# A retention block feeding a gated MLP on one core: the first unit in two parts, a 128-row product for the decay rows, and another order of the first block with more work on GpSimd

## The chip, the cores and the metric

The kernel runs on one core of one Trainium2 chip. The metric is the time of one execution on the device in microseconds (us); the times given are medians of several runs. A profile is one further execution recorded by the hardware profiler. Its engines are PE (TensorE matmuls; PEld are its weight loads), DVE (VectorE), ACT (ScalarE), POOL (GpSimd) and SP (SyncE, which here only issues transfers). Each engine works through its own instructions in order.

## The reference

```python
# q, k, v: (4, 8, 768, 64) float32
gamma = 1.0 - 2.0 ** (-5.0 - np.arange(H))
for t in range(S):
    state = gamma[None, :, None, None] * state + einsum('bhd,bhe->bhde', k[:, :, t], v[:, :, t])
    y[:, :, t] = (1 / np.sqrt(D)) * einsum('bhd,bhde->bhe', q[:, :, t], state)
x = y.transpose(0, 2, 1, 3).reshape(3072, 512)      # one row per token
h = x @ w_in                                        # w_in (512, 2048), w_out (2048, 512)
return (h * (1.0 / (1.0 + np.exp(-1.702 * h)))) @ w_out
```

The recurrence over 768 tokens per head, with a decay per head, is followed by an MLP with a sigmoid-gated hidden layer. All is float32; the two weight matrices arrive as 64-bit words (float64) and are narrowed to float32 on the chip.

## The kernel before

**Retention in steps.** Tokens are worked in steps of 64, for two batches at once and all 8 heads; a step is written with its number, `j`. For a step, q and k are turned on PE by an identity product (`turn_q`, `turn_k`, L283; the copies out of PSUM are `turned_q`, `turned2_q`, `turned_k`, L300). `score` (L339) forms the products of keys and queries, `masked` (L380, VectorE) multiplies them with a mask of decays, `gain` (L347) forms the step's own addition to the state from the decayed keys (`decay`: L318 on GpSimd, or L323 on ScalarE in eight instructions, one per head), `past` (L358) the part of the old state, and `own` (L367) the part of the step itself. `state` (by_state, L387) and `x` (output, L409) put both parts together into the MLP's input, in the tile X. `aged` (L418 on VectorE or GpSimd, L421 on ScalarE in four instructions) and `updated` (L432) carry the state on. Four steps make a block of MLP rows; the first eight steps, two blocks, are what the change concerns.

**Weights.** Each 128-column pair of `w_in` comes in as two halves of raw 64-bit words by SyncE (`w3a`, `w3b`; L201) into a ring of three slots, and is narrowed by six works: `abs` (L237) and `low` (L241) on ScalarE, `clip` (L245), `lift` (L248), `sign` (L253) and `rest` (L258) on VectorE. A slot of the ring is loaded again when `low` and `sign` of its last weight are done. `w0` to `w7` are of `w_in`, `w8` to `w15` of `w_out`.

**The MLP of the first block.** A unit `up0.th.p` (up0, L476) is the product of weight pair `p` with half `th` of the block's rows: eight matmuls of 256 columns. Half 0 is the rows of steps 0 and 1, half 1 those of steps 2 and 3, so the unit waits for `x1` or `x3`. `gate` (hidden, L457) is ScalarE's sigmoid product. Later units of block 0 (`zero`, L559) and block 1 (`seven`, L599) use a scheme of seven products with sums of the operands: `zero_x` (L546) and `seven_x` (L500) make four sums of X each, one building on another, on VectorE; `seven_4`, `seven_6`, `seven_52` make the sums of weights, and `seven_keep` (L538) writes some of them to DRAM on SyncE's queue.

**The order.** All these works stand in one list of names (L1105 to L1127). `works[name]` issues the work, a suffix as `@pool` names the engine, and within each engine the instructions run in the order of the list (`pin` keeps it, L124). SyncE's and GpSimd's transfers stand in their queues in the same order, and a transfer into a buffer that is still read waits there and holds all behind it. `zN` is `N` dummy matmuls of 512 bfloat16 columns (keep_warm, L1011) whose results nobody reads. `rows` (L1017) spreads the row of decays over 128 partitions by one matmul with a column of ones: one partition of `ones` (L104) times one partition of `row` (L103). `mask`, `causal` and `rowd` are made from its result. `table` loads ScalarE's table for the sigmoid. From the third block on, the loop at L1138 orders the work; the change does not touch it.

## Time and profile before

| | us |
|---|---|
| median of 3 runs | 649.44 (648.33 to 653.43) |
| the profiled execution | 651.44 |
| its span, first to last instruction | 649.7 |
| PE busy | 633.4 |
| VectorE busy | 435.6 |
| ScalarE busy | 184.4 |
| GpSimd busy | 152.0 |

The span is counted from the first instruction; the execution's own time has 1.74 us around it. Busy time is the union of an engine's instructions. A matmul of float32 appears as two passes, so a unit of eight matmuls shows as x16. "Idle before" with a releaser tells what an engine waited for, as far as the semaphores show it. The granted clock of TensorE stands in the column PEclk of a table of stretches; 1.00 there also stands for stretches without a record of the clock.

### The profile page before, as it was taken

The numbers are of one execution on the slowest core, as the hardware profiler recorded it, in microseconds if no ns is written. First come the engines' busy times: TensorE is split into PE (matmuls) and PEld (weight loads), VectorE is DVE, ScalarE is ACT, GpSimd is POOL, SyncE is SP. The second block draws the span as 40 slices with busy tenths as digits, with TensorE's granted clock in tenths as the row PEclk, the third lists the DMA queues.
The fourth block names the chain that finished last, engine by engine and source line by source line (L and its number), as shares of the span: only waits on it lengthen the run. The fifth ranks groups of instructions, "written<-read, shape, count | busy, mean of one in ns | idle before, by whom it ended". The sixth has DMA issues, their size and how long they took to land.

```text
span 649.7 us, 15510 instructions
## 1 busy us (share of the span) xinstructions
PE 633.4 (97%) x6543; PEld 578.4 (89%) x6543; DVE 435.6 (67%) x643; ACT 184.4 (28%) x329; POOL 152.0 (23%) x184
## 2 busy tenths in 40 slices
PE   7899999999999998999999999999999999999997
PEld 4788888888889997889999889999888999888997
DVE  2879887979989962438874337985246976145854
ACT  3778237661001102332101333100333110233210
POOL 4000211300612435000645000635300425200000
PEclk9989999999999999999999999999999999999999
DMA  9995587783368875720667730667741354221143
GB/s 198 228 258 161 112 252 214 198 209 57 93 200 264 206 175 171 200 67 4 172 179 213 215 85 1 160 161 189 211 95 49 89 174 143 110 91 49 59 153 98
DMA packets 150710, 96.86 MB, mean 149 GB/s; under 512 B 130512, under 2 KB 135888, under 8 KB 149616
## 3 DMA queue, kind: packets, MB, share of 16 engines
q1 hardware_dynamic: 138048, 42.83, 30.2%
q0 software_dynamic: 8672, 40.00, 19.3%
q10 hardware_dynamic: 3920, 13.04, 5.4%
q8 instruction: 51, 0.84, 0.6%
q14 instruction: 19, 0.16, 0.1%
HBM read 79.18 MB, written 14.94 MB: 145 GB/s over the span
## 4 chain that ended last, share of the span: by engine, by line
PE 83%; DMA 9%; SPq 5%; issue 1%; DVE 1%; ACT 1%; ACTq 0%
PE pq L821 33%; PE px L698 17%; PE pz L698 9%; PE pd L954 7%; PE ph L599 6%; PE py L698 4%; DMA W<-in_moe_w_out_dram 2%; SPq L161 2%; PE pa L339 2%; DMA q_in<-in_q_dram 2%; DMA kn_in<-in_k_dram 2%; DMA LATE<-W1D 1%; SPq L176 1%; PE py L367 1%; PE pa L347 1%; DMA v_in<-in_v_dram 1%
## 5 line engine op out<-in xcount | busy, mean ns | idle before, releaser
L821 PE MATMUL pq<-W,G 128*128 128x128 f32 x840 | 100.3, 276 | 0.0
L821 PEld LDWEIGHTS pq<-W,G 128*128 128x128 f32 x840 | 97.0, 192 | 0.8
L796 POOL DMA_DIRECT2D LATE<-W2D x34 | 18.7, 551 | 260.5 <-PE pq L821 139.8
L821 PE MATMUL pq<-LATE 128*128 128x128 f32 x560 | 74.8, 277 | 0.0
L821 PEld LDWEIGHTS pq<-LATE 128*128 128x128 f32 x560 | 68.2, 192 | 0.6
L698 PE MATMUL px<-X,LATE 128*128 128x256 f32 x256 | 60.6, 380 | 2.2 <-DMA LATE<-W1D 2.2
L698 PE MATMUL px<-X,W1A 128*128 128x256 f32 x256 | 60.5, 379 | 0.0
L698 PEld LDWEIGHTS px<-X,LATE 128*128 128x128 f32 x256 | 48.6, 190 | 9.1 <-issue 2.6
L698 PEld LDWEIGHTS px<-X,W1A 128*128 128x128 f32 x256 | 48.4, 190 | 6.3
L743 DVE TENSOR_TENSOR G<-pz,vv 128x512 f32<-128x512 f32 x16 | 11.1, 692 | 51.5 <-ACT vv L713 51.5
L843 ACT ACTIVATE o<-pq 128x512 f32<-128x512 f32 (+1 forms) x18 | 9.8, 544 | 119.9 <-PE pq L821 94.3
L457 ACT ACTIVATE G<-G 128x512 f32<-128x512 f32 x49 | 30.9, 630 | 43.1 <-DVE G L753 19.7
L821 PE MATMUL pq<-LATE,G 128*128 128x128 f32 x280 | 37.0, 275 | 0.0
L821 PE MATMUL pq<-W,LATE 128*128 128x128 f32 x280 | 37.0, 275 | 0.0
L954 PE MATMUL pd<-W,LATE 128*128 128x256 f32 x160 | 35.1, 380 | 0.0
L821 PEld LDWEIGHTS pq<-W,LATE 128*128 128x128 f32 x280 | 34.1, 192 | 0.0
L821 PEld LDWEIGHTS pq<-LATE,G 128*128 128x128 f32 x280 | 34.1, 192 | 0.0
L954 PEld LDWEIGHTS pd<-W,LATE 128*128 128x128 f32 x160 | 30.4, 190 | 4.1
L683 DVE TENSOR_TENSOR G<-G 128x512 f32<-128x512 f32 (+2 forms) x28 | 15.9, 567 | 23.5 <-ACT G L457 23.5
L810 DVE TENSOR_TENSOR LATE<-G 128x512 f32<-128x512 f32 x35 | 27.6, 789 | 5.0 <-PE pq L821 2.2
L476 PE MATMUL ph<-X,W1A 128*128 128x256 f32 x128 | 30.6, 397 | 0.2 <-DVE X L409 0.2
L698 PE MATMUL pz<-X,W1A 128*128 128x256 f32 x128 | 30.3, 380 | 0.0
(214 smaller groups left out, 1163.5 us busy)
## 6 DMA issues: line engine op xcount, KB each, us to landing
LATE<-W2D POOLq DMA_DIRECT2D x34, 768.0 KB, 5.2
W<-in_moe_w_out_dram SPq DMA_DIRECT2D x12, 512.0 KB, 6.0
LATE<-W1D ACTq DMA_DIRECT2D x4, 1536.0 KB, 9.7
LATE<-W1D POOLq DMA_DIRECT2D x4, 1536.0 KB, 8.9
kn_in<-in_k_dram SPq DMA_DIRECT2D x84, 64.0 KB, 4.8
W<-in_moe_w_in_dram SPq DMA_DIRECT2D x10, 512.0 KB, 4.8
out_dram<-o POOLq DMA_DIRECT2D x20, 256.0 KB, 4.6
q_sq<-in_q_dram SPq DMA_DIRECT2D x144, 32.0 KB, 3.0
```

Source lines behind the costliest of these rows:

```text
L161: keep(engine.dma_start(t[r * D:(r + 1) * D, i * HP:(i + 1) * HP], src[b + i, r * HP:(r + 1) * HP, rows, :].rearrange("h p d -> p h d")))
L339: pe.matmul(PAS[HALF[w], u, 0, s, :], kt[HALF[u], w, s, :], qt[HALF[u], w, s, :], start=True, stop=True)
L457: pin(act.activation(g, h[:, i], AF.Gelu_apprx_sigmoid))
L476: pe.matmul(h[:, ab], w, X[:, 2 * th + c // 2, c % 2, :], start=(ab == 0 and c == 0), stop=(c == 3), skip_group_check=True)
L599: pe.matmul(acc[:, u, :], w, x, start=(start and u == 0 and c == 0), stop=(stop and c == 1), skip_group_check=True)
L683: hold(dve.tensor_sub(q[0][1], q[0][0], q[0][1]))
L698: pe.matmul(acc[:, u, :], w1(2 * d + u, sw)[:, c, :], X[:, sx, c, :], start=(start and u == 0 and c == 0), stop=(stop and c == 1), skip_gr ...
L743: dve.tensor_add(a[3], z, v)
L796: engine.dma_start(c, W2D[i])
L810: dve.tensor_add(d[:, 0], s2, a11)
L821: pe.matmul(p0[:, j, :], a[:, d], w[:, d], start=(new and j == 0 and d == 0), stop=(d == NP // 2 - 1), skip_group_check=True)
L954: pe.matmul(p0[:, n, :], g1(m, p, sa)[:, n * P:(n + 1) * P], W2[:, sb, p, :], start=(new and p == 0 and n == 0), stop=(last and p == NP - ...
```

## The change

- The first unit, `up0.0.2`, is cut by steps. `firstb` and `firsta` (new function `up0_first`) multiply the rows of step 0 alone with the second and the first halves of the weight pair, 64 columns for each of two batches, eight matmuls of 128 columns. `up0.0.2` itself does the same for step 1. Both go into the same PSUM tile.
- `row` and `ones` have 128 partitions. Two blocks of G are set to zero first, and the row is loaded into partition 0, so that the product in `rows` contracts over 128 partitions of which 127 add zeros.
- The order of the list is another one, above all in its first third. q0 is issued first; `rows` stands behind `turn_k0`; `z5` becomes `z4` behind `turn_q0`, and `z1 z4` are added ahead of `own1`; `mask` and `causal` stand behind `turn_q1`; w0b goes ahead of q1, k3 ahead of v2, w3a ahead of q3; w11a goes behind `seven_keep.2`, and `updated7` some way back.
- Engines: `decay0` from GpSimd to ScalarE; `decay2` to `decay5` from ScalarE to GpSimd; `aged2` from VectorE and `aged4` from ScalarE to GpSimd; `aged5` from ScalarE to VectorE; `zero_x` and `seven_x` from VectorE to GpSimd; `rowd` from ScalarE to VectorE; `updated0` and `turned2_q1` from VectorE to ScalarE.

The new words `both` and the tuple of engines in `load` are not used by the list. In the instruction streams both parts of the first unit stand directly behind one another on PE, behind `turn_q2`, and ScalarE has a table load ahead of its first copy as well as the one of `table`.

```diff
@@ -100,8 +100,8 @@
     G0 = one.tile([P, 2, TH], F32, name="g0", tag="kd")
     X1 = W2[:, 6].rearrange("p (s c) t -> p s c t", s=4)
     rowd = const.tile([P, HP, D], F32, name="rowd")
-    row = G[0:1, 4, 0:2].rearrange("p a (h t) -> p (a h) t", t=D)
-    ones = G[0:1, 4, 2, 0:P]
+    row = G[:, 4, 0:2].rearrange("p a (h t) -> p (a h) t", t=D)
+    ones = G[:, 4, 2, 0:P]
     cold = const.tile([P, 2 * H], F32, name="cold")
     whole = const.tile([P, HP], F32, name="whole")
     whole_h = const.tile([P, H], F32, name="whole_h")
@@ -155,7 +155,8 @@
                 if j < NEW:
                     to, at = t[i * D:(i + 1) * D], src[b + i, :, rows, :].rearrange("h p d -> p h d")
                     for n in range(1 if name == "v" else 2):
-                        keep(engine.dma_start(*((to, at) if name == "v" else (to[:, n:H:2], at[:, n * HP:(n + 1) * HP]))))
+                        by = engine[n] if isinstance(engine, tuple) else engine
+                        keep(by.dma_start(*((to, at) if name == "v" else (to[:, n:H:2], at[:, n * HP:(n + 1) * HP]))))
                 else:
                     for r in range(2):
                         keep(engine.dma_start(t[r * D:(r + 1) * D, i * HP:(i + 1) * HP],
@@ -467,8 +468,25 @@
     def g1(m, p, s):
         return g(m, p // 2 * 2, s)[:, p % 2]
+    FIRST = []
+
+    def up0_first(half, t=0):
+
+        if not FIRST:
+            FIRST.append(ps.tile([P, 2, TH], F32, name="ph", tag="x"))
+        h = FIRST[0].rearrange("p ab (i t) -> p ab i t", i=2)
+        x = X.rearrange("p s c (i t) -> p s c i t", i=2)
+        for ab in range(2):
+            for c in (2, 3) if half else (0, 1):
+                pe.matmul(h[:, ab, :, t:t + D], W1A[:, 2, 2 * ab + half, c % 2, :], x[:, half, c % 2, :, t:t + D],
+                          start=(t == 0 and half == 1 and ab == 0 and c == 2), stop=(half == 0 and c == 1), skip_group_check=True)
+
     def up0(th, p, tag):
+        if (th, p) == (0, 2):
+            for half in (1, 0):
+                up0_first(half, D)
+            return W1L[:, p, 0:2].rearrange("p s c f -> p (s c f)"), FIRST[0]
         h = ps.tile([P, 2, TH], F32, name="ph", tag=tag)
         for ab in range(2):
             for c in range(4):
@@ -491,13 +509,13 @@
     SUM_X, SUM_W = {}, {}
-    def seven_x():
+    def seven_x(engine=dve):
         for n, tag in ((4, "q_sq"), (5, "q_sq"), (6, "k_sq"), (2, "k_sq")):
             SUM_X[n] = two.tile([P, 2, TH], F32, name=f"x{n}", tag=tag)
         for to, a, b in ((SUM_X[4], X1[:, 2], X1[:, 0]), (SUM_X[5], X1[:, 3], SUM_X[4]),
                          (SUM_X[6], X1[:, 3], X1[:, 2]), (SUM_X[2], X1[:, 1], SUM_X[5])):
-            pin(dve.tensor_sub(to, a, b))
+            pin(engine.tensor_sub(to, a, b))
     def seven_4(d):
@@ -540,10 +558,10 @@
     SUM_0 = {n: W2[:, i, NP - 2:NP] for i, n in enumerate((4, 5, 6, 2))}
-    def zero_x():
+    def zero_x(engine=dve):
         for n, a, b in ((4, X[:, 2], X[:, 0]), (5, X[:, 3], SUM_0[4]), (6, X[:, 3], X[:, 2]), (2, X[:, 1], SUM_0[5])):
-            pin(dve.tensor_sub(SUM_0[n], a, b))
+            pin(engine.tensor_sub(SUM_0[n], a, b))
     ZERO = {}
@@ -1003,6 +1021,7 @@
                 bass.AP(tensor=col_decay.tensor, offset=col_decay.offset, ap=[[W, D], [D * W + H, 2], [1, H]])))
         make_identity(nc, ident)
         dve.memset(flow, 1.0)
+        dve.memset(G[:, 4, 0:2], 0.0)
         dve.memset(ones, 1.0)
         dve.memset(first, 0.0)
@@ -1057,7 +1076,7 @@
         "table": lambda: pin(act.activation(first, first, AF.Gelu_apprx_sigmoid)),
         "mask": lambda: pin(dve.tensor_mul(m3, products["rows"], cold[:, 0:H, None].to_broadcast([P, H, D]))),
-        "causal": causal, "rows": rows, "row": lambda engine=pool: pin(engine.dma_start(row, row_decay[None, :, 0:D])),
+        "causal": causal, "rows": rows, "row": lambda engine=pool: pin(engine.dma_start(row[0:1], row_decay[None, :, 0:D])),
         "rowd": lay_rowd, "whole": lay_whole, "late_loads": late_loads, "anew": halves_anew,
         } | {f"z{n}": lambda n=n: keep_warm(n) for n in range(1, 33)}
     for j in range(2 * CB):
@@ -1070,6 +1089,7 @@
         works[f"turned2_q{j}"] = lambda *e, j=j: turned(j, 0, *(e or (act,)), 1)
         works |= {f"turned_{name}{j}": lambda *e, j=j, n=n: turned(j, n, *e) for n, name in enumerate("qk")}
     works |= {f"pace{n}": lambda n=n: PACE.append(n) for n in range(1, 17)}
+    works |= {"firstb": lambda: up0_first(1), "firsta": lambda: up0_first(0)}
     works |= {"seven_x": seven_x, "zero_x": zero_x}
     for d in range(NP // 2):
         works |= {f"seven_{n}.{d}": lambda d=d, do=do: do(d)
@@ -1103,31 +1123,32 @@
     begin()
     for name in """
-        row@sp k0@act table q0 v0 z5 rows turn_q0 turn_k0 q1 w0b k1@sp w0a mask causal turned_q0
-        turned2_q0@dve turned_k0 decay0@pool score0 v1 turn_k1 turn_q1 masked0 gain0 turned_k1 turned_q1 turned2_q1@dve own0 abs0b low0b updated0
-        decay1@pool score1 clip0b lift0b sign0b rowd whole q2 k2@sp masked1 abs0a low0a rest0b x0 past1 gain1
-        clip0a lift0a sign0a own1 rest0a aged1 turn_k2 turn_q2 w2b w2a state1 updated1 x1 turned_k2 turned_q2 turned2_q2@dve
-        v2 q3 k3@sp up0.0.2 score2 abs2 decay2 aged2@dve q4 clip2 lift2 sign2 low2 decay3 w3b w3a
-        masked2 turn_k3 turn_q3 k4@sp gain2 past2 own2 v3 q5 rest2 k5@sp gate0.0.2 turned_k3 turned_q3 turned2_q3@dve updated2
-        state2 score3 decay4 low3 turn_q4 turn_k4 up0.0.3 x2 masked3 gain3 past3 own3 abs3 clip3 lift3 sign3
-        turned_q4 turned2_q4@dve rest3 turned_k4 score4 turn_k5 turn_q5 up0.0.6 w1a w5b w1b aged3 updated3 state3 w5a v4
-        x3 up0.1.3 turned_q5 turned2_q5@dve gate0.0.3 abs1 low1 abs5 clip1 aged4 lift1 sign1 masked4 own4 gain4 w6a
-        rest1 clip5 lift5 gate0.0.6 sign5 up0.0.7 past4 w6b decay5 low5 rest5 updated4 v5 gain5 w4a abs6
-        gate0.1.3 turned_k5 clip6 state4 x4 lift6 score5 masked5 w4b abs4 up0.1.7 low6 aged5 gate0.0.7 w7a w7b
-        low7 low4 q6 sign6 v6 own5 rest6 past5 seven_4.2 state5 gate0.1.7 seven_6.2 updated5 zero2.0 clip4 up0.1.6
-        lift4 sign4 x5 seven_52.2 rest4 turn6 anew decay6 abs7 aged6 up0.1.2 w8a gate0.1.2 clip7 zero_x zero2.1
...
-        w9a updated6 aged7 gate0.1.6 zero2.5 decay7 zero2.6 state6 w11a seven_4.0 x6 zero0.0 score7 masked7 abs8 clip8
-        past7 zero0.1 state7 seven_6.0 seven_52.0 lift8 sign8 gain7 own7 x7 seven_x zero0.2 zero0.3 zero0.4 zero0.5 low8
-        seven_keep.2 w9b abs9 low11 clip9 rest8 lift9 zero0.6 w10a seven2.0 w10b seven2.1 abs11 clip11 lift11 sign11
...
+        k0@act whole q0 row@sp v0 w0b q1 turn_q0 z4 turn_k0 rows k1@sp w0a turned_q0 table turned2_q0@dve
+        turned_k0 decay0@act score0 v1 turn_k1 turn_q1 mask causal masked0 abs0b gain0 low0b clip0b lift0b sign0b turned_k1
+        turned_q1 turned2_q1@act own0 rest0b updated0@act decay1@pool score1 rowd@dve q2 k2@sp masked1 x0 gain1 low0a z1 z4
+        own1 abs0a clip0a lift0a sign0a rest0a aged1 turn_k2 past1 turn_q2 w2b w2a state1 x1 k3@sp firstb
+        firsta up0.0.2 updated1 turned_k2 turned_q2 turned2_q2@dve v2 w3a q3 decay2@pool aged2@pool q4 score2 abs2 clip2 lift2
+        sign2 low2 turn_k3 turn_q3 k4@sp decay3@pool w3b masked2 gain2 past2 own2 v3 q5 rest2 k5@sp gate0.0.2
+        turned_q3 turned_k3 turned2_q3@dve updated2 decay4@pool state2 low3 turn_q4 turn_k4 score3 up0.0.3 x2 masked3 gain3 past3 abs3
+        clip3 lift3 sign3 turned_q4 turned2_q4@dve rest3 turned_k4 score4 own3 turn_k5 turn_q5 up0.0.6 w1a w5b w1b aged3
+        updated3 state3 w5a v4 x3 zero_x@pool up0.1.3 turned_q5@act gate0.0.3 turned2_q5@dve abs1 abs5 clip1 aged4@pool low1 lift1
+        sign1 masked4 own4 gain4 w6a rest1 clip5 lift5 low5 gate0.0.6 sign5 up0.0.7 past4 decay5@pool rest5 updated4
+        w6b v5 gain5 w4a abs6 turned_k5 clip6 state4 gate0.1.3 x4 lift6 score5 masked5 w4b gate0.0.7 abs4
+        up0.1.7 aged5@dve w7a low6 w7b low7 low4 q6 sign6 v6 own5 rest6 past5 seven_4.2 gate0.1.7 seven_6.2
+        state5 zero2.0 clip4 up0.1.6 lift4 updated5 sign4 x5 seven_52.2 rest4 abs7 turn6 anew decay6 aged6 up0.1.2
...
+        w11b zero2.3 zero2.4 turn7 w9a updated6 gate0.1.6 aged7 zero2.5 decay7 zero2.6 state6 x6 seven_4.0 zero0.0 score7
+        masked7 abs8 clip8 past7 zero0.1 state7 seven_6.0 seven_52.0 lift8 sign8 gain7 own7 x7 seven_x@pool zero0.2 zero0.3
+        zero0.4 zero0.5 low8 seven_keep.2 w11a low11 w9b abs9 clip9 rest8 lift9 zero0.6 w10a seven2.0 w10b seven2.1
...
-        works[name](*[{"sp": sp, "pool": pool, "act": act, "dve": dve}[x] for x in e])
+        works[name](*[{"sp": sp, "pool": pool, "act": act, "dve": dve, "both": (act, sp)}[x] for x in e])
```

More of the change, by code (lines that the diff above doesn't have):

```diff
@@ L1115 @@
-        rest1 clip5 lift5 gate0.0.6 sign5 up0.0.7 past4 w6b decay5 low5 rest5 updated4 v5 gain5 w4a abs6
-        gate0.1.3 turned_k5 clip6 state4 x4 lift6 score5 masked5 w4b abs4 up0.1.7 low6 aged5 gate0.0.7 w7a w7b
-        low7 low4 q6 sign6 v6 own5 rest6 past5 seven_4.2 state5 gate0.1.7 seven_6.2 updated5 zero2.0 clip4 up0.1.6
-        lift4 sign4 x5 seven_52.2 rest4 turn6 anew decay6 abs7 aged6 up0.1.2 w8a gate0.1.2 clip7 zero_x zero2.1
-        score6 past6 q7 w8b v7 zero2.2 masked6 lift7 sign7 gain6 rest7 own6 w11b zero2.3 zero2.4 turn7
@@ L1120 @@
-        w9a updated6 aged7 gate0.1.6 zero2.5 decay7 zero2.6 state6 w11a seven_4.0 x6 zero0.0 score7 masked7 abs8 clip8
-        past7 zero0.1 state7 seven_6.0 seven_52.0 lift8 sign8 gain7 own7 x7 seven_x zero0.2 zero0.3 zero0.4 zero0.5 low8
-        seven_keep.2 w9b abs9 low11 clip9 rest8 lift9 zero0.6 w10a seven2.0 w10b seven2.1 abs11 clip11 lift11 sign11
-        seven_4.1 rest11 seven2.2 abs10 seven2.3 seven2.4 seven_w.1 clip10 lift10 sign9 seven0.0 seven2.5 low10 low9 rest9 sign10
-        updated7 rest10 seven_4.3 seven2.6 seven0.1 seven0.2 seven0.3 seven0.4 seven1.0 seven_keep.0 w14b w14a w12b w12a abs12 seven_w.3
@@ L1125 @@
-        clip12 seven0.5 seven0.6 seven_v.1 lift12 sign12 abs14 clip14 low12 rest12 lift14 sign14 seven1.1 seven1.2 w13a seven1.3
-        w13b abs13 low14 seven_v.3 clip13 lift13 seven1.4 sign13 seven3.0 seven1.5 rest14 seven1.6 seven3.1 seven3.2 seven3.3 seven3.4
-        w15a seven_keep.3 seven_keep.1 w15b abs15 clip15 lift15 low13 low15 sign15 seven3.5 rest13 seven3.6 rest15 late_loads
+        k0@act whole q0 row@sp v0 w0b q1 turn_q0 z4 turn_k0 rows k1@sp w0a turned_q0 table turned2_q0@dve
@@ new lines @@
+        w6b v5 gain5 w4a abs6 turned_k5 clip6 state4 gate0.1.3 x4 lift6 score5 masked5 w4b gate0.0.7 abs4
+        up0.1.7 aged5@dve w7a low6 w7b low7 low4 q6 sign6 v6 own5 rest6 past5 seven_4.2 gate0.1.7 seven_6.2
+        state5 zero2.0 clip4 up0.1.6 lift4 updated5 sign4 x5 seven_52.2 rest4 abs7 turn6 anew decay6 aged6 up0.1.2
+        w8a gate0.1.2 clip7 zero2.1 score6 past6 q7 w8b v7 zero2.2 masked6 own6 lift7 sign7 gain6 rest7
+        w11b zero2.3 zero2.4 turn7 w9a updated6 gate0.1.6 aged7 zero2.5 decay7 zero2.6 state6 x6 seven_4.0 zero0.0 score7
@@ new lines @@
+        masked7 abs8 clip8 past7 zero0.1 state7 seven_6.0 seven_52.0 lift8 sign8 gain7 own7 x7 seven_x@pool zero0.2 zero0.3
+        zero0.4 zero0.5 low8 seven_keep.2 w11a low11 w9b abs9 clip9 rest8 lift9 zero0.6 w10a seven2.0 w10b seven2.1
+        abs11 clip11 lift11 sign11 seven_4.1 rest11 seven2.2 abs10 seven2.3 seven2.4 seven_w.1 clip10 lift10 sign9 seven0.0 seven2.5
+        low10 low9 rest9 sign10 rest10 seven_4.3 seven2.6 seven0.1 seven0.2 seven0.3 seven0.4 seven1.0 seven_keep.0 w14b w14a w12b
@@ L1128 @@
+        w12a abs12 seven_w.3 clip12 updated7 seven0.5 seven0.6 seven_v.1 lift12 low12 sign12 abs14 clip14 lift14 rest12 sign14
+        seven1.1 seven1.2 w13a seven1.3 w13b abs13 low14 seven_v.3 clip13 lift13 seven1.4 sign13 seven3.0 seven1.5 rest14 seven1.6
+        seven3.1 seven3.2 seven3.3 seven3.4 w15a seven_keep.3 seven_keep.1 w15b abs15 clip15 lift15 low13 low15 sign15 seven3.5 rest13
+        seven3.6 rest15 late_loads
     """.split():
         name, *e = name.split("@")
-        works[name](*[{"sp": sp, "pool": pool, "act": act, "dve": dve}[x] for x in e])
+        works[name](*[{"sp": sp, "pool": pool, "act": act, "dve": dve, "both": (act, sp)}[x] for x in e])
```

## The prediction

> **What bounds the kernel now.** I read the page first, then a table of busy time in short stretches, the matmul engine's waits, the chain of waits, and the timeline of the first 110 us.
>
> ```profile
> span 649.7 us, 15510 instructions
> PE 633.4 (97%) x6543; PEld 578.4 (89%) x6543; DVE 435.6 (67%) x643; ACT 184.4 (28%) x329; POOL 152.0 (23%) x184
> ```
>
> TensorE is 97% busy, so all idle time together is 16 us. A change of orders can win no more than that, plus what a lowered clock costs. The stretches show where it lies:
>
> ```profile
> core 0: us, PE busy (x) PEld busy (x) DVE busy (x) ACT busy (x) POOL busy (x), PEclk, DMA share, GB/s
> ...
> 20.00:25.00 5.00, 4.82 (x76) 4.14 (x69) 4.06 (x9) 1.94 (x4) 0.00 (x0) 1.00 1.05 160
> 25.00:30.00 5.00, 5.00 (x83) 4.15 (x85) 4.87 (x8) 5.00 (x17) 0.00 (x0) 1.00 0.92 279
> 30.00:35.00 5.00, 2.28 (x116) 2.11 (x108) 3.34 (x7) 4.26 (x15) 0.00 (x0) 0.99 1.15 180
> 35.00:40.00 5.00, 5.00 (x20) 4.32 (x19) 3.51 (x7) 4.46 (x9) 0.00 (x0) 0.67 0.96 310
> ...
> 50.00:55.00 5.00, 5.00 (x83) 4.22 (x82) 4.79 (x7) 5.00 (x14) 0.41 (x1) 1.00 0.73 218
> 55.00:60.00 5.00, 5.00 (x113) 4.27 (x112) 4.97 (x9) 4.62 (x9) 0.79 (x1) 1.00 0.87 250
> ```
>
> The hole is at 30 to 35, where PE works 2.28 of 5 us; behind it the granted clock is 0.67. From 40 on PE has no hole, but VectorE is full too (4.97 of 5). The waits and the timeline name the hole:
>
> ```profile
> PE pa L339 <- ACT G L323: 2.7, 1, 2.7
> ...
> PE ph L599 <- ACT p L604: 0.6, 1, 0.6
> PE ph L559 <- DVE W L546: 0.5, 1, 0.5
> ```
>
> ```profile
> 32.75 2.21 ACT L323 ACTIVATE G<-kn_in,cold 128x64 f32<-128x64 f32 x8 [0.63 <-DMA kn_in<-in_k_dram]
> ...
> 33.88 0.69 PE L339 MATMUL pa<-G 64*64 64x64 f32 x32 [2.72 <-ACT G L323]
> ...
> 35.92 4.82 PE L476 MATMUL ph<-X,W1A 128*128 128x256 f32 x16
> ```
>
> ScalarE's decay of a key block (L323, eight instructions) sits in its queue waiting for a load, and score3 waits. The unit after it takes 4.82 us for 16 passes; the same unit takes 3.72 at 51.72. Later rows:
>
> ```profile
> 50.90 0.69 DVE L245 TENSOR_SCALAR G<-G 128x1024 f32<-128x1024 f32 x1
> ...
> 61.67 1.99 PE L559 MATMUL ph<-X,W1A 128*128 128x256 f32 x8
> ...
> 70.92 1.04 POOL L423 TENSOR_TENSOR state<-state,whole_h 128x512 f32<-128x512 f32 x1
> ...
> 71.29 1.22 DVE L245 TENSOR_SCALAR G<-G 128x1024 f32<-128x1024 f32 x1
> ```
>
> VectorE runs without a gap from 46.38 (clip1) past 73. Its rest6 ends at 61.54, and zero2.0 on PE starts at 61.67: VectorE and PE are level. The last two rows matter most: the same VectorE instruction takes 0.69 us alone and 1.22 beside a GpSimd product. And the chain:
>
> ```profile
> 54.12 5.13 DMA G<-in_moe_w_in_dram
> ...
> 89.87 9.48 DMA W<-in_moe_w_out_dram
> ```
>
> SyncE's queue, released at 53.71 by VectorE's sign5, leads through issue after issue to a landing at 99.36, to p on ScalarE and to PE at 103.12. From there PE is unbroken but for a 2.2 us wait on its own reload, so a lead at 103 arrives at the end.
>
> **The change, part by part.** Passes at the low early clock cost twice (a transpose 223 ns against 109 to 127).
>
> *Start (to 16 us).* SyncE issues q0 first, so turn_q0 starts about 0.9 us earlier (5.4). The row product now stands behind turn_k0. Bounds for its two passes: 0.86 us (two warm-up passes of 0.42) to 2.04 (L1020 before); I take 1.7, four times a cold 256-column pass of 0.43. Score0 then ends near 12.2 (10.81 before), still about when k1 lands (12.06, plus some 0.5 because w0b now goes ahead of q1). Mask and causal move behind rows: 11.1 + 0.69 + 2 x 0.66 gives masked0 at 13.9 (11.63); own0 needs it only behind turn_k1, turn_q1 and gain0, at 15.5 (14.98). The 128x512 memset (about 0.54 by the 0.27 of 128x256) holds the row load to 1.8 us, and SyncE behind it; rows runs at 9.3, so the load is covered. Decay0 on ScalarE costs 2.0 (L323) and ends before gain0. A second table load (1.28) lies in ScalarE's wait for turn_k0; uncovered it would cost 1.28. `whole` ahead of causal costs GpSimd 1.1 us while it waits for the mask. Part: -0.5.
>
> *First unit (16 to 27 us).* turned2_q1 and updated0 go to ScalarE, rowd to VectorE (2 x 0.43): score1 near 16.4 (16.76). Five more dummy passes stand before own1: 2.1 us cold, of which masked1 (18.25) would have cost some 0.7 anyway. The unit's first half no longer waits for x1. It costs 16 passes of 128 columns (112 ns each in the later L821 rows, so 1.8 us), and the halves sum to one whole unit: no work added. I get its end at 26.8 (27.92), a lead of 1.0, bounds 0 and 2 by how early the clock rises.
>
> *Decays off ScalarE (25 to 42 us).* decay2 to decay5 took 2.01, 2.04, 2.21 and 2.05 us there; on GpSimd 1.04 each (L318). The 2.72 wait goes. Late next are loads: k3's four issues (2.5 us) go ahead of v2, and w3a ahead of q3; q3 lands near 26.8, k4 near 31 (32.65). Score3 at about 32 (33.88), the second unit 32 to 35.5 at full clock (ended 40.74), rest3 near 38.7, and the third unit at 39.3 instead of 43.62: a lead of 4.3. w1 and w5 follow k5 on SyncE, issued from 31.7 (34.20), landing near 41 (44.59): clip1 at 42.1 instead of 46.38, the same 4.3. Bounds 1.7 (w1 gains only its issue's 2.5 less 0.8) to 6.
>
> *VectorE against GpSimd (42 to 62 us).* zero_x (4), aged4 and decay5 now run on GpSimd as soon as x3 is out, that is, beside clip1 to rest5. Nearest rows: POOL L423 at 70.92 cost VectorE 0.53, at 117.40 0.84; L423 at 83.82 and L325 at 69.55 and 86.70 cost it nothing, mean 0.27. The cheap ones met masks, state and transposes; here about four fifths of VectorE's work is clip, lift, sign and rest. I take 0.5 per operation: five ahead of sign5 cost 2.5, six ahead of rest6 3.0; bounds 0.27 and 1.04. aged5, now VectorE's, adds 0.65 ahead of rest6. Lead at sign5: 4.3 - 2.5 = 1.8. Lead at rest6: 4.3 - 0.65 - 3.0 = 0.65.
>
> [...]
>
> *To the end.* zero_x is out of the way of zero2.2, so its 0.5 wait goes: PE leads by 1.2 at 73.9. seven_x off VectorE (4 x 0.69) was not on the path. w11a goes behind seven_keep's three issues (1.5 us), ahead of w9b still, and low11 ahead of abs9: p needs both either way, so nothing. PE had 0.6 to spare before p, so p sets the end: its lead is sign5's, 1.8.
>
> **Sum.** Span 649.7 - 1.8 = 647.9. The profiled execution took 651.44, 1.74 over its span and 2.0 over the median of the three runs, 649.44. On that median: 649.44 - 1.8 = 647.6.
>
> **The rivals.**
> 1. *More gain.* GpSimd's operations cost VectorE the mean row, 0.27: leads 4.3 - 1.35 = 2.95 at sign5, or with the upper bound 6 nearly 4.6. For: ScalarE loses 8 us of work. Against: VectorE is full. Time 645 to 646.5.
> 2. [...] At 1.04 for each of six and 0.65 for aged5, VectorE loses 6.9 against 4.3: zero2.0 starts 2.6 late, time 652.0. It decides once an operation costs over 0.61, (4.3 - 0.65) / 6. For: 0.84 at 117.40. [...]
> 3. *The transfers set the pace.* DMA share is 0.92 to 1.15 from 20 to 40; if w1 still lands at 44.59, clip1 keeps 46.38. zero_x then falls into VectorE's idle time and only aged4 and decay5 cost, 1.0: time about 650.4. Against: the share has 160 to 310 GB/s in it, so there is room.
> 4. *The clock falls again* while PE waits for q3 and k4 near 27 to 31: 1.7 us off the lead (16 passes, 4.82 against 3.72, and turn_k4, 0.85 against 0.49, are 1.5 of it): time 649.3.
>
> **How the numbers follow.** My forecast (646.5 to 649) 0.40; rival 1 0.22; rivals 3 and 4 together 0.20; rival 2 0.14; something unseen 0.04. The range 643 to 652.5 takes in all four rivals. About 1%, 6.5 us, is what a measurement of this kernel can tell from no change: under 643 lies 0.08, from the top of rival 1 and the unseen; over 655.9 lies 0.04; between, 0.88.
>
> **What would show it.** Right: no L323 block ahead of score3; no clock below 1 near 35 to 38; third unit near 39; POOL rows L564 beside VectorE rows over 0.69 us. Wrong: clip1 still at 46, VectorE at unchanged durations, a new PE wait on q3 or k4 over 2 us, or PE at 103 ahead by much more or less than 1.8.

## The result and the profile after

The changed kernel takes 656.28 us (median of 15 runs, 653.81 to 661.47); the kernel before, run beside it on the same chip, 650.87 us (15 runs, 647.59 to 655.62). The ratio is 1.0091, 95% interval 1.0070 to 1.0112: about 5.9 us slower by the ratio (the two medians are 5.4 us apart), where 1.8 us faster was forecast, and outside the forecast range of 643 to 652.5. The profiled execution took 661.47 us, the longest of its 15; a second profile, of an execution of 657.99 us, is read beside it.

The page of the changed kernel, as for the kernel before:

```profile
span 659.7 us, 15525 instructions
PE 634.5 (96%) x6563; PEld 578.3 (88%) x6563; DVE 437.9 (66%) x635; ACT 178.3 (27%) x299; POOL 168.6 (26%) x197
```

PE's work is the same within 1.1 us, the span 10 us longer: the change made idle time. ScalarE lost 6 us of work, GpSimd won 17. The same stretches of the changed kernel:

```profile
core 0: us, PE busy (x) PEld busy (x) DVE busy (x) ACT busy (x) POOL busy (x), PEclk, DMA share, GB/s
...
30.00:35.00 5.00, 3.40 (x128) 3.05 (x118) 4.88 (x8) 2.84 (x6) 1.25 (x2) 1.00 0.91 225
35.00:40.00 5.00, 2.91 (x42) 2.15 (x41) 4.90 (x8) 3.45 (x8) 0.00 (x0) 0.87 1.12 294
50.00:55.00 5.00, 3.83 (x18) 3.04 (x16) 4.93 (x4) 3.47 (x4) 5.00 (x4) 1.00 0.03 5
55.00:60.00 5.00, 3.44 (x75) 3.08 (x76) 4.90 (x7) 2.20 (x4) 2.57 (x4) 1.00 0.64 206
```

The hole that was at 30 to 35 (2.28 of 5) is smaller there, has a second half at 35 to 40, and there are two new ones from 50 to 60, where PE had none. At 50 to 60 VectorE is as full as before, but with 11 instructions instead of 16, and GpSimd is busy 7.6 us beside it. PE's waits give each hole a name:

```profile
...
PE pt L284 <- DMA kn_in<-in_k_dram: 3.7, 1, 3.7
PE pa L348 <- issue: 2.8, 3, 1.6
PE py L368 <- DVE G L381: 2.5, 1, 2.5
PE ph L494 <- issue: 2.1, 1, 2.1
PE ph L617 <- DVE G L663: 2.0, 1, 2.0
...
PE ph L577 <- DVE w L535: 0.5, 1, 0.5
...
```

The wait for ScalarE's L323 (2.7) and that for zero_x (0.5) are gone, as forecast. New are own4's wait for `masked4` (L381), a stop inside the second unit that no semaphore explains (L494), and a wait for VectorE's L663 late in `seven` (L617). The second profile has the same three: 2.4, 1.5 and 2.0 us. (The longest wait of L348, gain2 at 32.88, ends as masked2 on VectorE ends, at 32.77.) The chain of waits takes in the same places: 2.06 us of `issue` at 36.67, sign1 on VectorE (L254) at 52.50, lift12 (L249) at 132.01.

gain2 starts 0.1 us behind masked2's end in the kernel before too (29.54 and 29.44), so masked2 is what it waits for, and masked2 is late in part because of lift2, which stands ahead of it in VectorE's queue. In the kernel before, and then in the changed kernel:

```profile
26.69 0.69 DVE L248 TENSOR_SCALAR G<-G 128x1024 uint32<-128x1024 uint32 x1
```

```profile
28.68 1.49 POOL L319 TENSOR_TENSOR G<-kn_in,cold 128x512 f32<-128x512 f32 x1
...
29.31 1.41 DVE L249 TENSOR_SCALAR G<-G 128x1024 uint32<-128x1024 uint32 x1
```

The GpSimd row is decay2, which the change moved there; lift2 takes 0.72 us longer beside it.

Where PE stands at the same work, in us from the start of the span (the fourth column is an experiment, below):

| | before | changed | changed, 2nd | decays alone |
|---|---|---|---|---|
| own0 | 14.98 | 15.34 | 15.64 | 14.89 |
| second unit starts | 35.92 | 36.19 | 35.08 | 33.97 |
| third unit | 43.62 | 46.76 | 44.78 | 40.48 |
| clip1 (VectorE) | 46.38 | 49.88 | 47.89 | 43.98 |
| zero2.0 | 61.67 | 68.13 | 66.02 | 59.14 |
| the product that needs p | 103.12 | 109.20 | 106.81 | 101.78 |
| end of block 1's units | 148.11 | 158.09 | 155.68 | 146.78 |

So the lag is 0.3 or less at the start of the second unit, 1.2 to 3.1 behind it, 4.4 to 6.5 at zero2.0 and 7.6 to 10.0 at 148: it grows in three places. In the timeline of the changed kernel, the first is this:

```profile
36.19 0.48 PE L494 MATMUL ph<-X,W1A 128*128 128x256 f32 x1
38.72 0.59 PE L494 MATMUL ph<-X,W1A 128*128 128x256 f32 x1 [2.06 <-issue]
```

One pass, 2.06 us of nothing, and then passes that start 0.43 us apart, until 42.1, instead of 0.22: the granted clock is 0.62 over 38 to 42.5. The second, on VectorE, first in the kernel before and then in the changed one with GpSimd beside it:

```profile
46.38 0.70 DVE L245 TENSOR_SCALAR G<-G 128x1024 f32<-128x1024 f32 x1 [0.57 <-ACT G L237]
47.11 0.69 DVE L248 TENSOR_SCALAR G<-G 128x1024 uint32<-128x1024 uint32 x1
47.84 1.29 DVE L253 SCALAR_TENSOR_TENSOR G<-W,G 128x512 uint32<-128x512 uint32 x2
49.16 0.69 DVE L380 TENSOR_TENSOR G<-pa,mask 128x512 f32<-128x512 f32 x1
```

```profile
49.88 0.90 DVE L246 TENSOR_SCALAR G<-G 128x1024 f32<-128x1024 f32 x1 [0.80 <-ACT G L238]
50.81 1.66 DVE L249 TENSOR_SCALAR G<-G 128x1024 uint32<-128x1024 uint32 x1
52.50 3.09 DVE L254 SCALAR_TENSOR_TENSOR G<-W,G 128x512 uint32<-128x512 uint32 x2
55.62 0.69 DVE L381 TENSOR_TENSOR G<-pa,mask 128x512 f32<-128x512 f32 x1
```

```profile
50.17 1.74 POOL L564 TENSOR_TENSOR W<-X 128x512 f32<-128x512 f32 x1
51.87 1.72 POOL L564 TENSOR_TENSOR W<-X,W 128x512 f32<-128x512 f32 x1
53.56 1.48 POOL L419 TENSOR_TENSOR state<-state,whole 128x512 f32<-128x512 f32 x1
```

From clip1 to the start of masked4 are 5.74 us; before they were 2.78 (46.38 to 49.16), with lift at 0.69 instead of 1.66. masked4, for which own4 waits on PE, stands behind them in VectorE's queue. The third, with lift12 in the kernel before ahead of it:

```profile
125.34 0.84 DVE L248 TENSOR_SCALAR X<-X 128x1024 uint32<-128x1024 uint32 x1
```

```profile
130.72 0.68 DVE L433 TENSOR_TENSOR state<-state,pa 128x512 f32<-128x512 f32 x1
...
131.92 2.72 DVE L249 TENSOR_SCALAR X<-X 128x1024 uint32<-128x1024 uint32 x1
132.19 1.89 POOL L424 TENSOR_TENSOR state<-state,whole_h 128x512 f32<-128x512 f32 x1
```

`updated7` (L433) stands behind clip12 now. It costs VectorE 0.6 us there, and it releases GpSimd's L424, which falls beside lift12: 2.72 us instead of 0.84. PE comes to the end of this at 144.21, after 2.04 us of waiting, with a granted clock of 0.57 over 144 to 148. The prediction never priced this move.

### The profile page after: what moved, and what is told of

Read it like the earlier page. It is cut to its first block, busy times and chain, and to the rows that moved or that the text cites. A ratio compares the mean times of both kernels' runs of the same rounds, so it can differ in the third digit from the quotient of the medians.

```text
span 659.7 us, 15525 instructions
## 1 busy us (share of the span) xinstructions
PE 634.5 (96%) x6563; PEld 578.3 (88%) x6563; DVE 437.9 (66%) x635; ACT 178.3 (27%) x299; POOL 168.6 (26%) x197
## 4 chain that ended last, share of the span: by engine, by line
PE 72%; DMA 13%; DVE 5%; SPq 5%; issue 2%; ACT 1%; POOL 0%; DVEq 0%; POOLq 0%; ACTq 0%
PE pq L839 24%; PE px L716 16%; PE pz L716 8%; PE pd L972 6%; PE ph L617 5%; PE py L716 4%; SPq L177 3%; DMA LATE<-W1D 2%; DMA kn_in<-in_k_dram 2%; DMA v_in<-in_v_dram 2%; DMA k_sq<-in_k_dram 2%; PE pa L340 1%; PE ph L577 1%; SPq L162 1%; DMA W2D<-LATE 1%
## 5 line engine op out<-in xcount | busy, mean ns | idle before, releaser
L716 PE MATMUL pz<-X,LATE 128*128 128x256 f32 x128 | 30.2, 379 | 0.0
```

Of the source, the lines that this page charges most:

```text
L716: pe.matmul(acc[:, u, :], w1(2 * d + u, sw)[:, c, :], X[:, sx, c, :], start=(start and u == 0 and c == 0), stop=(stop and c == 1), skip_gr ...
```

## The experiments

Ratios are to the kernel before, run beside each, with 95% intervals; 0.001 of a ratio is 0.65 us. The labels a_ and b_ are of kernels made from the changed one and from the one before.

**1. The forecast gain alone.** The kernel before with

```diff
-decay2 ... decay3 ... decay4 ... decay5
+decay2@pool ... decay3@pool ... decay4@pool ... decay5@pool
```

> The kernel before with one part of the change alone: decay2 to decay5 on GpSimd instead of ScalarE; all else as before. The prediction's theory (the ScalarE decay ahead of score3 costs a wait and a cooled clock, and a lead won there arrives at the end): no 2.7 us wait of score3 on ScalarE, the third unit at 39.5 to 42 instead of 43.62, clip1 earlier by as much, and the time 1.5 to 4 us under the kernel before, ratio 0.994 to 0.998. Rival (the loads pace this stretch, and the wait only changes its name): the third unit within 0.7 us of 43.6, time within 0.7 us. Second rival (GpSimd's products slow VectorE's clip, lift and sign beside them): VectorE rows beside L318 at 1.2 us instead of 0.69, time 0.5 to 2 us over the kernel before.

Measured: ratio 1.0002 (0.9982 to 1.0022). Its timeline:

```profile
33.97 3.62 PE L476 MATMUL ph<-X,W1A 128*128 128x256 f32 x16
...
40.48 0.81 PE L476 MATMUL ph<-X,W1A 128*128 128x256 f32 x3
...
72.33 0.92 PE L559 MATMUL ph<-W,w 128*128 128x256 f32 x3 [1.48 <-DVE W L546]
```

The mechanism is as predicted: no wait for ScalarE, the second unit in 3.6 us at full clock, the third unit 3.1 us earlier. But the lead is 2.4 at clip1 (VectorE waits 1.3 us there for abs1, which waits for w1), 2.5 at zero2.0, and 1.3 at the product that needs p, because zero2.2 now waits 1.48 us for zero_x instead of 0.50 and PE then waits for p. 1.3 us would be a ratio of 0.998, just outside the interval, and this profile is of the fastest of the 12 executions (647.90 us, median 649.93): the step exists, and by itself it is worth 1.2 us at most. The second rival's mechanism is there too, though not its price: sign2 on VectorE takes 2.01 us beside decay2 on GpSimd, instead of 1.29.

**2. The later GpSimd operations undone, and made alone.** In the changed kernel (a_dve):

```diff
-x3 zero_x@pool ... clip1 aged4@pool ... past4 decay5@pool ... aged5@dve ... clip7 zero2.1
+x3 ... clip1 aged4 ... past4 decay5 ... aged5 ... clip7 zero_x zero2.1
```

> The changed kernel with the later moves to GpSimd undone: zero_x on VectorE at its old place behind clip7, aged4, aged5 and decay5 on ScalarE; the start and decay2 to decay4 stay changed. Theory of contention (six GpSimd operations beside clip1 to rest6 cost VectorE about 0.5 us each, and VectorE is on the path): clip1 to masked4 back from 5.74 to about 2.8 us, the lag behind the kernel before at zero2.0 falls from 6.5 to about 3.5, time 2.5 to 3.5 us under the changed kernel (lag 5.4 becomes 2 to 3 us). Rival (PE is late by its own waits and VectorE only follows): VectorE's rows get shorter but the lag at zero2.0 stays over 5.5, time within 1 us of the changed kernel.

And in the kernel before, zero_x, aged4 and decay5 alone moved the other way (b_zerox):

> The kernel before with zero_x on GpSimd behind x3 and aged4 and decay5 on GpSimd, six GpSimd operations in all beside clip1 to rest6; all else as before. [...] Rival (VectorE has room there): own4's wait under 0.5 us and the time within 0.7 us.

Measured: 1.0054 (1.0029 to 1.0080) against 1.0091 for the changed kernel, 2.4 us less; and 1.0049 (1.0031 to 1.0067), 3.2 us over the kernel before. Its timeline is the changed kernel's:

```profile
46.62 0.69 DVE L245 TENSOR_SCALAR G<-G 128x1024 f32<-128x1024 f32 x1 [0.59 <-ACT G L237]
46.64 1.82 POOL L546 TENSOR_TENSOR W<-X,W 128x512 f32<-128x512 f32 x1
47.34 1.66 DVE L248 TENSOR_SCALAR G<-G 128x1024 uint32<-128x1024 uint32 x1
...
52.39 0.69 DVE L380 TENSOR_TENSOR G<-pa,mask 128x512 f32<-128x512 f32 x1
```

masked4 starts 5.77 us behind clip1, own4 waits 2.23 us for it, zero2.0 comes at 66.09 instead of 61.67. In the first of the two kernels masked4 starts 2.78 us behind clip1, as before the change. Over all 20 profiles of this document that distance is 5.60 to 5.81 us in the six with these GpSimd operations, and 2.78 or 2.79 in the fourteen without. The theory of contention holds, with 2.4 us in the first kernel, where 2.5 to 3.5 were expected, and 3.2 in the second. It is the largest single part that was undone and made alone. (The first kernel has aged5 back on ScalarE as well; the second never moved it.)

**3. updated7.** Moved back in the changed kernel (a_upd7), and moved alone in the kernel before (b_upd7):

```diff
-sign10 rest10 ... clip12 updated7 seven0.5
+sign10 updated7 rest10 ... clip12 seven0.5
```

> The changed kernel with updated7 alone back between sign10 and rest10, where it stood before. Theory (moved behind clip12, updated7 takes 0.6 us of VectorE there and releases the GpSimd product L424 just beside lift12, which takes 2.7 us instead of 0.85; VectorE then keeps PE waiting 2.05 us at 144): no wait of L617 on VectorE L663, no clock under 1 behind it; time 2 to 3.9 us under the changed kernel, about half of its lag behind the kernel before. Rival (seven_x on GpSimd or w11a and low11 make VectorE late there): the wait stays over 1 us and the time within 1 us of the changed kernel.

> The kernel before with updated7 alone moved behind clip12, as the change has it. Theory as for the run with it moved back: lift12 at about 2.7 us beside the GpSimd product L423, a new wait of L599 on VectorE of about 2 us between 130 and 145, time 2 to 3.9 us over the kernel before. Rival (that wait needs the lateness of the changed kernel's first third): no wait over 0.5 us there, time within 1 us of the kernel before.

Measured: 1.0068 (1.0044 to 1.0091), 1.5 us less than the changed kernel; and 1.0027 (1.0011 to 1.0043), 1.8 us over the kernel before. The second has the pair of rows again:

```profile
126.26 2.71 DVE L248 TENSOR_SCALAR X<-X 128x1024 uint32<-128x1024 uint32 x1
126.54 1.88 POOL L423 TENSOR_TENSOR state<-state,whole_h 128x512 f32<-128x512 f32 x1
```

and PE's wait for L645 behind it, 1.77 us. So the cause is shown, at a little less than the 2 to 3.9 us expected. In the first the wait for L663 goes, but another takes its place: 1.6 us for a reload of W1A. That wait was first met here.

**4. Both undone (a_fix: the edits of 2 and 3 in the changed kernel), and the first unit whole as well (a_fix_whole).**

```diff
-x1 k3@sp firstb firsta up0.0.2
+x1 k3@sp up0.0.2
...
-        if (th, p) == (0, 2):
-            for half in (1, 0):
-                up0_first(half, D)
...
```

> The changed kernel with both later costs undone at once: updated7 back behind sign10, and zero_x, aged4, aged5 and decay5 off GpSimd as in the kernel before. The start, the first unit in two parts, decay2 to decay4 on GpSimd and seven_x on GpSimd stay. Theory (the two costs add up, 2.4 to 3.2 and 1.5 to 1.8 us, and the rest of the change is worth about nothing): time 1 to 2 us over the kernel before, ratio 1.001 to 1.003. Rival (they overlap, because what one gives back is lost at the next wait): ratio 1.004 or more, as with zero_x alone undone.

> As the run before it, and besides the first unit whole again behind x1: 32 entries less in PE's instruction stream ahead of the second unit. Theory (the stop inside the second unit is the block of instructions that begins with the 961st entry and comes late): that entry now lies behind the second unit, which takes 3.5 to 3.7 us without a stop; no issue wait over 0.3 us inside it, and no clock under 1 behind 35 us; the first unit starts later by up to 1.5 us for waiting on x1; time 0 to 2 us under the run before it. Rival (the stop comes from what the unit reads): the second unit stops as before, 1 to 3 us.

Measured: 1.0029 (1.0011 to 1.0047) and 1.0059 (1.0037 to 1.0080). The two costs add up (2.4 and 1.5 us; 4.0 together). The second unit of the first kernel, and then of the second:

```profile
33.69 0.48 PE L494 MATMUL ph<-X,W1A 128*128 128x256 f32 x1
36.50 3.40 PE L494 MATMUL ph<-X,W1A 128*128 128x256 f32 x15 [2.33 <-issue]
```

```profile
33.39 3.72 PE L490 MATMUL ph<-X,W1A 128*128 128x256 f32 x16
...
39.89 0.99 PE L340 MATMUL pa<-G 64*64 64x64 f32 x30 [1.68 <-DVE G L301]
```

With 32 entries less in PE's stream the stop is gone from the second unit, so it is no matter of what the unit reads. The time did not fall for it, against the expectation; with the unit whole it rose by about 1.9 us (the two medians are 1.84 apart, the intervals just overlap). PE waits 1.68 us for VectorE's copies (L301) six microseconds later. That this wait is the whole of the loss is not shown: the profile is of an execution 2.5 us under that kernel's median.

**5. Is the stop a block of instructions that comes late?** All nine profiles of kernels made from the changed one with the unit in two parts show the stop at the same place: counting all of PE's rows in the trace from the start (matmuls, weight loads, and its sequencer's semaphore rows, 24 by then), at entry 961 or 962, for 1.2 to 3.4 us, whatever the transfers or dummies. Six of the nine stop again at 1217 or 1218, for 0.5 to 2.2 us: 256 entries on. The page counts the transfers that bring instructions:

```profile
q8 instruction: 51, 0.84, 0.5%
```

51 of 16 KB each (51 x 256 is 13056, and PE has 13214 rows, so this queue is taken to be PE's); in all these versions one starts 2.7 to 3.3 us before the stop at 961 ends. In the kernel before one starts at 31.17, when PE waits anyway. Two kernels were made on experiment 1: with the first unit in two parts (b_decays_split, 32 more entries), and with 14 unread matmuls of 8 columns ahead of turn_k1 on top (b_tiny, 28 more).

```diff
-v2 q3 k3@sp up0.0.2
+v2 q3 k3@sp firstb firsta up0.0.2
...
-score0 v1 turn_k1
+score0 v1 tiny turn_k1
+    def tiny(n):
+        x = flow.bitcast(mybir.dt.bfloat16)
+        for _ in range(n):
+            pe.matmul(idle[:, 0:8], x[:, 0:P], x[:, 0:8], start=True, stop=True)
```

> The kernel before with decay2 to decay5 on GpSimd, and besides the first unit in two parts of steps directly behind one another, which is 32 more entries in PE's instruction stream for the same work. To be read beside the run with the decays alone. Theory (PE's instructions come in blocks of 256; when the 256 ahead of the 962nd entry are used up in less than about 5.5 us the next block is not there, and the second unit stops inside): a wait of 1 to 2.3 us put down to issue at the 962nd entry, inside the second unit near 35 us, with a lower clock behind it, and none in the run with the decays alone; third unit 1 to 4 us later than there, time 0.5 to 3 us over it. Rival (the stops of the changed kernel come from its transfers or its order): no wait over 0.3 us inside the second unit, third unit within 0.5 us of 40.5.

> The kernel before with decay2 to decay5 on GpSimd and the first unit in two parts, and 14 matmuls of 8 columns ahead of turn_k1, where PE waits for k1 anyway: 28 more entries in PE's stream and no other work; nobody reads them. Theory of blocks: the 961st entry, 0.0 to 0.2 us from being late in the run without them, now lies in turn_q4 or turn_k4 ahead of the second unit, which PE wants at 33.4 and whose block comes at about 35.3: a wait of 1 to 2 us put down to issue there, the second unit later by as much, the third unit at 42 to 43 instead of 40.9. Rival: no such wait, third unit within 0.5 us of 40.9.

Measured: 0.9999 (0.9978 to 1.0021) and 1.0026 (1.0007 to 1.0045). The first has no stop, against the expectation: PE comes to entry 961 only at 35.3 us, inside its second unit, and a transfer of that queue had started at 32.33, 3.0 us ahead. Near turn_q4 the second has

```profile
34.27 0.69 PE L339 MATMUL pa<-G 64*64 64x64 f32 x32 [1.15 <-DVE state L432]
35.81 0.96 PE L283 MATMUL pt<-UB,q_in 128*128 128x128 f32 x4 [0.84 <-PE pa L339]
```

and that pass is entry 962. The stop came where it was foretold, at 0.84 instead of 1 to 2 us, with a clock below full behind it (the second unit takes 4.5 us). So the place of the stop goes with the number of entries, and its length with how soon the transfer starts: 1.2 to 3.7 us after PE passed entry 705, over all profiles, and 2.4 to 3.3 us more until PE goes on where it stops. My limit of 5.5 us for 256 entries was an estimate (in the changed kernel's first profile PE passed entry 705 at 33.04 and went on with entry 962 at 38.72, 5.7 us later) and too simple. That the transfer brings the entries for which PE stops is inferred from these times, from 16 KB and from the 256 entries; no run here tells how many such blocks PE holds.

**6. The start, the transfers, the dummies.** Four parts of the early change. The changed kernel without `z1 z4`; then with transfers in the old order:

```diff
-low0a z1 z4 own1
+low0a own1
```

```diff
-v0 w0b q1 turn_q0 ... x1 k3@sp firstb ... v2 w3a q3 decay2@pool ... w3b masked2
+v0 q1 w0b turn_q0 ... x1 firstb ... v2 q3 k3@sp decay2@pool ... w3b w3a masked2
```

> The changed kernel without the five dummy passes z1 z4 ahead of own1. Theory (they lie on the path, 2.25 us, with no other work behind which they hide): own1 starts 1.5 to 2.2 us earlier, masked1 being out at 19.0, and the lag at the first unit falls from 1.7 to about 0; time 1 to 2.2 us under the changed kernel if later loads do not take it back. Rival (they pay for themselves in the clock): without them the granted clock rises a window later and the first unit takes 5 to 7 us instead of 3.7, time 0 to 2 us over the changed kernel.

> The changed kernel with SyncE's transfers back in the old order at two places: q1 ahead of w0b, and v2, q3, k3 ahead of the weights w3b, w3a, which go behind again; no other engine's instructions move. Theory (the new order of the transfers holds up what PE needs first): the wait of turn_k1 on k1 falls from 3.7 to about 3 us, q3 lands 2 to 3 us earlier, gain2 and the second unit start 1 to 2 us earlier, time 1 to 2.5 us under the changed kernel. Rival (transfers are not what sets the pace before 40 us): PE's times at score0, own0, gain2 move by less than 0.5 us and the time stays within 0.7 us.

and the new start alone: the changed kernel's list up to own0 (`k0@act whole q0` to `turned2_q1@act own0`), then the remaining names in the order and on the engines of the kernel before, the first unit whole:

> The list of the change up to own0 and then the list before: q0 first, w0b ahead of q1, rows behind turn_k0 with its 128 rows, mask and causal behind turn_q1, decay0 and turned2_q1 on ScalarE; the first unit whole, everything behind own0 in the order and on the engines of the kernel before. Prediction's step (the start wins about 0.5 us): own0 within 0.6 us of 15.0 and the time within 0.7 us of the kernel before. Rival (k1, behind w0b, lands up to 1.4 us later and holds PE cold): turn_k1 at 12.5 to 13.6 instead of 12.2, the granted clock rises a window later, time 0.7 to 2 us over the kernel before.

Measured: 1.0095 (1.0068 to 1.0122), 1.0115 (1.0079 to 1.0152) and 0.9999 (0.9971 to 1.0027). None of these is where the time goes. The dummies and the transfers win nothing when undone: the second unit stops anyway and masked4 comes late anyway. The first unit starts at 22.47 without the dummies instead of at 25.89, but that is no effect of theirs that could be told: seven profiles that have the dummies and the same code up to there have it at 21.3 to 25.9. (For the window of the clock in two of these expectations the traces have 3.41 us: the granted clock was 0.50 from 34.93 to 38.34 in the profile of the kernel before, and from 14.84 to 25.08, three times as long, in the first of the changed kernel.) The start is worth nothing either way; own0 comes at 15.67 in its profile, which is of the slowest of its 12 executions (656.97, median 650.09).

**7. What is left.** With experiment 4 at 1.0029, the late part was taken apart. All named later moves undone in the changed kernel (`seven_x`, `w11a` and `low11` too: a_early), and those three made alone in the kernel before (the same lines the other way: b_late):

```diff
-state6 x6 seven_4.0 ... x7 seven_x@pool zero0.2 ... seven_keep.2 w11a low11 w9b abs9
+state6 w11a seven_4.0 x6 ... x7 seven_x zero0.2 ... seven_keep.2 w9b abs9 low11
```

> The changed kernel with all that lies behind 42 us undone: zero_x, aged4, aged5, decay5, updated7 as before, and also seven_x back on VectorE and w11a and low11 at their old places. Left are the start, the first unit in two parts and decay2 to decay4 on GpSimd. Theory early (the rest of 1.9 us lies before 42 us): ratio 1.002 to 1.004, as with seven_x on GpSimd; PE still stops inside the second unit. Theory late (it lies with seven_x, w11a and low11): the wait for the reload of W1A near 136 us (1.2 to 1.6 us) goes, time within 0.7 us of the kernel before.

> The kernel before with seven_x on GpSimd and w11a and low11 behind seven_keep.2, as the change has them, and nothing else. Theory late: a wait of PE for the reload of W1A near 136 us of 1 to 1.6 us, which the kernel before has not; the transfer lands 7.5 to 8.3 us after its issue instead of 6.3; time 1 to 2 us over the kernel before. Theory early: no such wait over 0.5 us and time within 0.7 us.

Measured: 1.0047 (1.0023 to 1.0070) and 0.9985 (0.9961 to 1.0010). The three cost nothing; the rest seemed to lie early. But a few reorderings had stayed in a_early against its description, among them `low12` ahead of sign12. Its transfers (issues, from the timeline), with PE's wait:

```profile
127.20 1.20 POOL L551 DMA_DIRECT2D W1A<-W1A  x1 [0.56 <-ACT W1A L550]
127.97 0.33 SPq L202 DMA_DIRECT2D W<-in_moe_w_out_dram  x1
...
135.02 1.99 PE L617 MATMUL py<-W,W1A 128*128 128x256 f32 x8 [1.16 <-DMA W1A<-W1A]
```

low12 frees the raw slot, and a weight load starts 0.8 us behind the reload of W1A instead of 1.8 (127.79 and 129.62 before); the reload lands 7.8 us after its issue instead of 6.3. Moved back there (a_low12), and moved alone in the kernel before, with lift14 ahead of rest12 as the change has it (b_low12):

```diff
-lift12 low12 sign12 abs14 clip14 lift14 rest12 sign14
+lift12 sign12 abs14 clip14 low12 rest12 lift14 sign14
```

> The run with the early part of the change, and besides low12 back behind clip14, so that the raw slot comes free and w13a is loaded as late as in the kernel before. Theory (w13a's load, 1.6 us earlier, takes bandwidth from the reload of W1A, which lands 7.8 us after its issue instead of 6.3, and PE waits 1.2 us for it): the reload lands within 6.7 us, the wait near 135 us goes, time 0.8 to 1.6 us under that run, ratio 1.002 to 1.0035. Rival (the rest lies before 42 us): the wait goes or not, the ratio stays at 1.004 to 1.007.

> The kernel before with low12 alone ahead of sign12, and with it lift14 ahead of rest12. Theory as in the run beside it: the reload of W1A lands 7.5 to 8.3 us after its issue, PE waits 0.8 to 1.6 us for it near 136 us, time 0.8 to 1.6 us over the kernel before. Rival: no wait over 0.3 us there and time within 0.6 us.

Measured: 1.0002 (0.9980 to 1.0024), and 1.0007 (0.9988 to 1.0027). In the first the order and the landing are as before, and the wait is gone:

```profile
129.09 1.20 POOL L551 DMA_DIRECT2D W1A<-W1A  x1 [0.56 <-ACT W1A L550]
130.93 0.33 SPq L202 DMA_DIRECT2D W<-in_moe_w_out_dram  x1
```

The second has the wait (1.36 us, the reload after 8.0 us), but its time is within the interval of no change. So the mechanism is shown and its size is not settled: 2.9 us by the one (interval of the difference about 0.8 to 5), 0.5 by the other (-0.8 to 1.8). In the changed kernel itself this wait does not occur. Its two profiles have the weight load 2.2 us behind the reload, which lands 4.5 and 4.6 us after its issue, and PE waits for VectorE's L663 instead; the wait comes up once `updated7` is back (1.6 us in experiment 3, 1.2 in the first kernel of experiment 4).

**8. A second profile, and a try at something better.** The latter is experiment 1 with

```diff
-x5 seven_52.2 rest4 ... clip7 zero_x zero2.1
+x5 zero_x seven_52.2 rest4 ... clip7 zero2.1
```

> The changed kernel once more, unchanged, for a second profile. If the lags in its first profile before 47 us (unit 2 at 36.2, third unit at 46.8) are that execution's own, the third unit comes at 43 to 45 here and the span is 652 to 656; own4's wait for masked4, 2.4 to 2.6 us, the stop inside the second unit, 1.2 to 3.4 us, and the wait of L617 near 140, 2.0 us, are there again. If they are the kernel's, the third unit is again at 46 to 47 and the span 658 or more.

> The kernel before with decay2 to decay5 on GpSimd, and zero_x on VectorE ahead of seven_52.2 and rest4 instead of behind clip7; a try at a version under both kernels. With the decays alone PE had 1.5 us of wait for zero_x at 72.3. Theory (the lead of 3 us won by the decays is lost at this wait and at p near 102): the wait goes, the lead at p grows from 1.3 to 2 to 3 us, time 1 to 2.5 us under the kernel before, ratio 0.996 to 0.9985. Rival (the transfers to p, not VectorE, take the lead back): PE waits at p instead, time within 0.7 us of the kernel before.

The second profile: third unit 44.78, span 656.2, the three waits there again (table above). Some 2 us of the lag at 47 in the first profile were that execution's own. The other: 1.0023 (0.9998 to 1.0048). Its wait for zero_x is gone, but PE stands 3.34 us at 73.33 for VectorE's transpose L294 (turn6), which zero_x pushed back. No version here is clear of the kernel before; the lowest ratio, 0.9985 in experiment 7, has 1 inside its interval.

## Why the prediction was wrong, by its own steps

- *Start, -0.5.* Right in being small: made alone, 0.9999. turn_q0 came at 4.78 (5.4 said). k1, where 0.5 us was allowed for w0b ahead of it, landed at 13.47 instead of 12.06 in this profile; turn_k1 started at 11.98 to 13.61 in the versions of the changed kernel, and at 12.03 to 13.29 in those made from the kernel before.
- *First unit, lead 1.0.* Right on the whole. Its end, 26.8 said, was 29.55 and 28.46 here, but these are the two latest of the seven profiles with the same code up to the third unit (a_dve, a_upd7, a_fix, a_early, a_low12 and the two of the changed kernel): 25.0 to 29.55, the middle one 27.1. How early the clock rises made the difference, as its bounds said: over 14 to 25 us the granted clock was 0.54 in the first profile and 1.00 in a_early, which came first. The dummies took 2.25 us cold, about the 2.1 allowed.
- *Decays off ScalarE, lead 4.3 at the third unit and at clip1.* **This is the step that failed.** The part that it describes was right: with the decays alone (experiment 1) the wait went, the clock was full, and the lead was 3.1 at the third unit and 2.4 at clip1. It left out two things. decay2 on GpSimd lengthens lift2 by 0.72 us, and masked2 behind it, for which gain2 waits 1.60 us in both profiles; the price of GpSimd's products was set only from 42 us on. And the second unit stops inside, at the entries of experiment 5, for 2.06 and 1.49 us in the two profiles, in the first with the clock halved behind it, so clip1 came 3.5 and 1.5 us late. The seven profiles put this in numbers. Their second unit starts at 31.6 to 36.2, the middle one 33.7, against 35.4 to 37.0, the middle one 35.9, in five profiles with the old code up to there (the kernel before, b_late, b_low12, b_upd7, b_zerox): a lead of 2.2 where 3.9 was said. Their third unit starts at 40.8 to 46.8, the middle one 44.2, against 43.1 to 43.8, the middle one 43.5: a lag of 0.7 where a lead of 4.3 was said. What the prediction asked of the profile, no clock under 1 near 35 to 38, was met to the letter and meant nothing: the clock fell at 38.7.
- *VectorE against GpSimd, 0.5 per operation.* Right in the sum, with some luck: 2.96 us from clip1 to masked4, where 3.0 was said for six operations. The first of the six ended ahead of clip1, so five cost about 0.6 each; in the second kernel of experiment 2 four cost 2.99 and the next one, decay5, 0.84 more on clip5 (1.53 us instead of 0.69). One of the prediction's rows was read too low: at 69.55 GpSimd's product did not cost nothing, rest4 (L258 at 68.65) took 1.42 us beside it, where rest1 took 1.22. No run of this stretch shows an operation at 1.04, the upper bound and rival 2's price: it was 0.6 to 0.84. Rival 2 put the point where this decides at 0.61, from the lead of 4.3. With no lead it decides at any price. The outcome is rival 2's wait, at about the price at which it was to decide.
- *The moves costed at nothing.* seven_x, w11a and low11: right (0.9985). zero_x's 0.5 wait went, as said; one of 0.5 for a sum of weights (`w`, L535) stands in its place.
- *Moves not costed at all.* updated7 (1.5 to 1.8 us) and low12 (0.5 to 2.9, once updated7 is back) are moved by the change and are in no term of the sum, so they were put at nothing without a reason; the description of the change does not name low12. The sentence that a lead at 103 arrives at the end left both out; from 103 to 148 the lag grew by 3.9 us in both profiles.

The sum as measured: early part to 42 us 0.1 (-1.3 to 1.6: a_low12, which keeps that part and the small reorderings, against the kernel before), GpSimd beside clip1 to rest6 2.4 to 3.2, updated7 1.5 to 1.8, low12 0.5 to 2.9: 4.5 to 8.0 against 5.9 measured. So the forecast's lead of 4.3 was worth nothing, its cost of 2.5 to 3.0 was there, and the two unpriced moves came on top. How far the stops cost time at the end of the run, and not only at the third unit, stays open: where the stop went (experiment 4) VectorE was late instead, and where one was added (b_tiny, experiment 5) the ratio rose by 0.0027, though the two intervals just overlap.

## What to carry to other kernels

A lead on the busiest engine is worth only what the next engine and the next load can follow: trace it from wait to wait before another cost is set against it. Cost every name that stands elsewhere in an order, also one "some way back": moving one VectorE instruction of 0.6 us cost 1.5 to 1.8, because of what it released beside which work. An engine whose work lengthens that of the full one (here 5.6 to 5.8 us for 2.8) is no free place for work. And count the entries of PE's stream: 32 less took a stop of 2.33 us out of the second unit (experiment 4), 28 more brought one of 0.84 us into turn_q4 (experiment 5).
